# Attention and MLP on one core: the first loads in a fixed order, and the first batch's keys and queries summed, scaled and split through TensorE and ScalarE

## The chip, the cores and the metric

The kernel runs on one core of a Trainium2 chip. The metric is the device time of one execution in microseconds (us), the median of several runs. One profiled execution gives the trace that is read here.

## The reference, cut to what matters

```
def _attn_ref(q, k, v):                     # 4 batches, 8 heads, 576 positions, 64 wide
    q_rot, k_rot = (rotate(q), rotate(k))   # [x1*cos - x2*sin, x1*sin + x2*cos]
    scores = scale * np.matmul(q_rot, k_rot.transpose(0, 1, 3, 2))
    ...                                     # softmax over the last axis
    return np.matmul(attn, v)

def _moe_ref(x, w_in, w_out):               # x: 2304 x 512, w_in: 512 x 2048, w_out: 2048 x 512
    h = x @ w_in
    g = np.where(pos, h, np.where(neg, 0.0, (h + beta) ** 2 / (4.0 * beta)))
    return g @ w_out
```

Keys and queries are rotated by their position, attention is taken for each batch and head, and its output, with the heads side by side, goes through a two-layer MLP.

## The kernel before

Every operand of a product is held as two f16 halves: `hi` is the scaled f32 value rounded to f16, `lo` is what is left. A product is three f16 matmuls (hi x hi, hi x lo, lo x hi). The halves are made by `split`: ScalarE (ACT) writes `hi` = scale * x, then VectorE (DVE) writes `lo` = scale * x - `hi`. The scale of a batch's keys and queries comes from a sum of squares: ACT squares a key tile (`add_square`), a one-column f32 matmul adds the partitions up (`root`), and some one-column DVE steps turn that into the factors (`factors`).

The rotation is done with two copies of each input that the host lays out: x, and x with its halves of 64 rolled. `turn` multiplies the first by the cosines, the second by the sines (both from the table `rt`), and adds the second to the first: three DVE instructions.

The first batch is prepared in four parts, `j` = 0 to 3, each a pair of heads: the keys are `rk[:, j]` (128 x 576, with the rolled copy in a stretch of `w` that is still free, called `first`), the queries `rq[:, j]` (128 x 256). From then on an item is one pair of heads by 128 query rows: 12 matmuls into `psS` (scores), two maxima on DVE (`mx`), two exponentials on ACT (`p`), then `hi` of the two probability tiles on ACT and `lo` on DVE (`phl`), a transposing DMA into `pT`, and later 28 matmuls per pair of items with the values (`psV`). The MLP follows block by block: `psH` from `w_in`, the activation on ACT and DVE (`a`, `r`, `g`), `psO` from `w_out`.

The 16 pieces of the two weight matrices arrive in a 64-bit format, 1 MB each. DVE puts each together with three instructions of 1024 columns (L493, L495, L497), ACT writes `hi`, and for the first five pairs of pieces TensorE (PE) and ACT make `lo`: an f32 matmul against the identity, a second one that subtracts `hi`, both in `psO` (L522, L523), and an ACT copy out of it (L526). The raw pieces use stretches of `w` itself, in the order of `rawseq`.

What order the instructions have on each engine is decided by `Plan.order`: each step has a cost, the steps are laid out in time engine by engine, and of the steps that are ready the one with the smallest rank goes first. The rank is a due time from `wanted`, moved by the table `SLACK` by group of steps. The plain loads go through the queue of SyncE (SP), with up to eight in flight, the raw weights through that of GpSimd (POOL).

Of the kernel before, what the change touches and what calls it, by code (L numbers as in the profile page):

```python
# [10 lines left out]
F32 = mybir.dt.float32  # L11
F16 = mybir.dt.float16
BF16 = mybir.dt.bfloat16
U32 = mybir.dt.uint32
AF = mybir.ActivationFunctionType
ALU = mybir.AluOpType
# [9 lines left out]
    "k0 dve": 41_100, "k0.00 dve": 46_400, "k1 act": 617_700, "k1 dve": 63_800, "k1.10 dve": 21_800,  # L26
    "k1.12 dve": 13_200, "k1.20 act": 39_400, "k1.20 dve": -4_900, "k1.30 dve": 385_800, "left0 act": -440_200,
    "left0 dve": -34_700, "left0.01 dve": 29_800, "left1 act": -682_100, "left1.20 dve": 4_500,
    "left1.22 dve": -1_000, "left1.32 pe": 57_700, "mlp0 act": -48_700, "mlp0 dve": -56_400, "mlp0 pe": 1_362_600,
    "mlp0.0.1 act": 186_100, "mlp0.0.2 act": 74_000, "mlp0.0.7 act": -87_400, "mlp1 dve": -637_500,  # L30
    "mlp1.1.2 act": -106_800, "mlp1.1.3 act": -122_000, "mlp2 act": -875_300, "mlp2 dve": 47_700,
    "mlp2 pe": 40_700, "mlp2.2.2 act": 1_200, "mlp2.2.3 pe": 45_800, "mlp2.2.4 dve": 63_100, "mlp3 act": -691_900,
    "mlp3 dve": -81_700, "mlp3 pe": -23_800, "mlp3.3.3 pe": 241_700, "mlp3.3.4 pe": 225_400,
    "mlp3.3.7 act": 43_400, "mlp3.3.7 pe": 162_900, "mlp3.4.2 pe": -800, "mlp3.5.1 pe": 65_600,
    "mlp3.5.2 dve": -202_300, "mlp3.5.2 pe": 29_400, "mlp3.5.7 pe": 34_500, "mlp3.6.1 pe": 20_600,
    "mlp3.6.2 pe": 25_500, "mlp3.6.7 pe": 163_600, "mlp3.7.0 pe": 82_200, "mlp3.7.3 pe": -15_800,
    "pv0 dve": -448_200, "pv0 pe": -769_100, "pv1 act": -1_444_600, "pv1 dve": -252_200, "pv1.123 pe": 71_100,
    "pv1.302 pe": -66_700, "q0 act": 100_000, "q0 dve": -18_900, "q0.001 act": -77_800, "q0.003 dve": 48_700,
    "q0.010 dve": 109_300, "q0.012 dve": 36_700, "q1 dve": 44_500, "q1.100 dve": -20_700, "q1.110 dve": 8_500,
    "q1.200 dve": -37_600, "q1.210 act": 52_900, "ql0 dve": -134_800, "ql1 dve": 190_900, "raw k0 sp": -12_600,  # L40
    "raw k0.00 sp": -14_800, "raw k0.01 sp": -368_000, "raw k0.02 sp": -12_000, "raw k0.03 sp": 11_100,
    "raw k1 sp": -1_486_700, "raw q0 sp": -6_000, "raw q0.000 sp": -9_500, "raw q0.002 sp": 50_400,
    "raw q0.003 sp": 221_800, "raw v0.0 sp": 71_700, "raw w.1 pool": -67_500, "s0 act": -70_500,
    "s0 dve": -190_500, "s0.001 dve": -66_100, "s0.003 dve": -18_000, "s0.021 dve": 65_100, "s0.022 act": 55_200,
    "s0.022 sp": 21_200, "s0.023 act": 27_000, "s0.031 act": -118_200, "s1 dve": -166_700, "s1 pe": -550_500,
    "s1.101 act": -14_300, "s1.102 act": -34_500, "s1.110 dve": -25_600, "s1.111 dve": -17_400,
    "s1.112 dve": -6_800, "s1.121 dve": 40_400, "s1.122 act": -77_600, "s1.123 act": -123_500,
# [15 lines left out]
class Plan:  # L63
# [59 lines left out]
    def order(self):  # L123
        steps, users = self.steps, self.users()
        n = len(steps)
        rank = [-1e9 if s[5].startswith("init") else x + SLACK.get(s[5], 0.0) + SLACK.get(s[8], 0.0) for x, s in zip(self.wanted(), steps)]
# [6 lines left out]
        def release(i):  # L133
            eng = steps[i][0]
            t = 0.0
            for d in steps[i][4]:
                by = steps[d][0]
                t = max(t, end[d] + (0.0 if by in DMA_ENGINES else 60.0 if by == eng else 205.0 if by == "pe" else 150.0))
            avail[i] = t + 60.0 * (eng in DMA_ENGINES)
            ready[eng].append(i)  # L140
# [43 lines left out]
def kernel(  # L184
# [63 lines left out]
    ndg = [xL_w[:, 256 + 128 * i:384 + 128 * i].bitcast(BF16) for i in range(2)]  # L248
    xL_keys = [("xL", l, e) for l in range(2) for e in range(2)]
# [6 lines left out]
    psO = [ps.tile([128, 512], F32, name=f"psO{i}") for i in range(2)]  # L256
# [24 lines left out]
    def dma(at, dst, src, r, w, nbytes, eng="sp"):  # L281
        q = nc.sync if eng == "sp" else nc.gpsimd
        plan.add(eng, 600.0 if eng == "sp" else 1000.0, at, lambda: q.dma_start(out=dst, in_=src), r, w, bw=nbytes / 300.0)
# [41 lines left out]
    def turn(at, x, xkeys, y, ykeys, p0, n, rep):  # L325
# [155 lines left out]
    def prep_w(which, c, at):  # L481
# [391 lines left out]
```

## Time and profile before

| | |
|---|---|
| median of 3 runs | 636.85 us (635.79 to 637.43) |
| the profiled execution | 636.13 us, of which its trace spans 634.4 us |
| PE busy | 559.6 us (88%) |
| DVE busy | 510.6 us (80%) |
| ACT busy | 441.5 us (70%) |
| DMA | 91.31 MB |

The profile lists each engine's busy time in the span and in 40 equal slices of it, the groups of instructions by line, what ended the idle time ahead of each instruction, and the chain of work that ended last. A busy PE counts matmuls at whatever clock they ran.

### The profile page before, as it was taken

What the parts mean: (1) busy time and instruction counts of PE and PEld (TensorE: products, weight loads), DVE (VectorE), ACT (ScalarE), POOL (GpSimd) and SP (SyncE); (2) the same over time, 40 slices, a digit from 0 to 9 for tenths busy, and PEclk for the clock granted to TensorE, in tenths of its full rate; (3) what the DMA queues carried; (4) which work ended last, traced back from release to release, by engine and by line L of the source; (5) the groups of instructions that cost most, each with busy time, mean ns of one, the idle gap of its engine ahead of it and who ended that gap; (6) DMA issues with size and microseconds to landing.
All of it is one profiled execution on the core that took longest, in us unless ns stands there. A gap on an engine that the chain in (4) does not pass through costs nothing.

```text
span 634.4 us, 12628 instructions
## 1 busy us (share of the span) xinstructions
PE 559.6 (88%) x5078; PEld 358.7 (57%) x5078; DVE 510.6 (80%) x839; ACT 441.5 (70%) x881; POOL 9.3 (1%) x22
## 2 busy tenths in 40 slices
PE   0146657999889899999999999999999999999996
PEld 0023223566565666665666666666666667666663
DVE  1999989999999899999899789968877684334332
ACT  1478768997989789998777799766777574223221
POOL 2000100000000000000000000000000000000000
PEclk9999788999999999999999999999999999999999
DMA  8997797828699968686668675666464664000000
GB/s 335 389 299 146 260 253 203 179 74 178 136 184 249 211 137 199 122 212 141 119 160 177 106 146 115 100 91 107 91 140 75 117 128 90 1 1 35 1 34 17
DMA packets 188009, 91.31 MB, mean 144 GB/s; under 512 B 170160, under 2 KB 178608, under 8 KB 185904
## 3 DMA queue, kind: packets, MB, share of 16 engines
q1 hardware_dynamic: 185648, 73.74, 55.7%
q0 software_dynamic: 2304, 16.78, 7.4%
q8 instruction: 39, 0.64, 0.4%
q14 instruction: 18, 0.15, 0.1%
HBM read 40.96 MB, written 4.72 MB: 72 GB/s over the span
## 4 chain that ended last, share of the span: by engine, by line
PE 54%; DVE 24%; DMA 11%; ACT 6%; issue 3%; SPq 0%; ACTq 0%; DVEq 0%
PE psO L709 20%; PE psH L679 20%; DMA pT<-phl 9%; PE psV L598 6%; DVE phl L555 5%; PE psS L569 5%; DVE mx L543 4%; ACT phl L553 2%; DMA rk<-in_km_dram 2%; ACT p L545 1%; PE psO L522 1%; DVE g L700 1%; PE psS L581 1%; DVE r L696 1%; DVE dup L330 1%
## 5 line engine op out<-in xcount | busy, mean ns | idle before, releaser
L709 PE MATMUL psO<-w,g 128*128 128x512 f16 x864 | 211.2, 380 | 1.2 <-ACT g L698 0.9
L679 PEld LDWEIGHTS <-w 128*128 128x128 f16 x1920 | 171.2, 98 | 48.2 <-issue 6.2
L679 PE MATMUL psH<-xT,w 128*128 128x256 f16 x1536 | 188.8, 273 | 3.2 <-ACT a L686 2.2
L555 DVE SCALAR_TENSOR_TENSOR phl<-p,sums,phl 128x576 f16<-128x576 f32 x144 | 113.4, 812 | 18.1 <-ACT phl L553 17.6
L553 ACT ACTIVATE phl<-p,sums 128x576 f16<-128x576 f32 x144 | 106.7, 766 | 30.6 <-DMA pT<-phl 17.3
L545 ACT ACTIVATE p<-psS,mx 128x576 f32<-128x576 f32 x144 | 105.4, 733 | 29.1 <-DVE mx L543 25.8
L709 PEld LDWEIGHTS <-g 128*128 128x128 f16 x864 | 78.8, 98 | 75.8 <-issue 3.2
L543 DVE TENSOR_REDUCE mx<-psS 128x1 f32<-128x576 f32 x144 | 103.8, 748 | 3.5 <-PE psS L569 2.2
L700 DVE SCALAR_TENSOR_TENSOR g<-r,g 128x512 f16<-128x512 f32 x72 | 49.4, 686 | 52.6 <-ACT g L698 51.5
L569 PE MATMUL psS<-kT,qT 64*128 64x512 f16 (+1 forms) x768 | 68.1, 300 | 19.5 <-ACT p L545 17.4
L686 ACT ACTIVATE a<-psH 128x512 f32<-128x512 f32 x72 | 42.4, 589 | 60.5 <-PE psH L679 60.1
L569 PEld LDWEIGHTS <-qT 64*128 64x128 f16 x768 | 32.5, 97 | 64.8 <-issue 43.4
L698 ACT ACTIVATE g<-r 128x512 f16<-128x512 f32 x72 | 44.9, 623 | 28.1 <-PE psO L709 17.1
L598 PE MATMUL psV<-pT,vS 128*64 128x256 f16 (+1 forms) x768 | 49.5, 251 | 4.1 <-DMA pT<-phl 4.1
L696 DVE SCALAR_TENSOR_TENSOR r<-a,r 128x512 f32<-128x512 f32 x72 | 49.5, 687 | 0.9
L689 DVE SCALAR_TENSOR_TENSOR r<-a 128x512 f32<-128x512 f32 x48 | 33.1, 689 | 19.7 <-ACT a L686 18.8
L598 PEld LDWEIGHTS <-vS 128*64 128x64 f16 x768 | 33.0, 111 | 16.0 <-issue 14.2
L298 PE MATMUL psV<-ssk,ones 128*128 128x1 f32 (+1 forms) x14 | 3.4, 314 | 29.3 <-ACT w L292 28.9
L598 PE MATMUL psV<-pT,vM 128*64 128x256 f16 (+1 forms) x480 | 28.5, 249 | 0.0
L545 ACT ACTIVATION_READ_ACCUMULATOR p<-psS,mx 128x1 f32 x144 | 28.0, 194 | 0.0
L679 PE MATMUL psH<-xL,w 128*128 128x128 f16 x384 | 26.2, 219 | 0.0
L598 PEld LDWEIGHTS <-vM 128*64 128x64 f16 x480 | 21.9, 112 | 0.1
(98 smaller groups left out, 476.7 us busy)
## 6 DMA issues: line engine op xcount, KB each, us to landing
w<-in_w_in_dram POOLq DMA_DIRECT2D x7, 1024.0 KB, 7.5
w<-in_w_out_dram POOLq DMA_DIRECT2D x6, 1024.0 KB, 7.9
rv<-in_vm_dram SPq DMA_DIRECT2D x8, 512.0 KB, 6.2
out_dram<-o SPq DMA_DIRECT2D x16, 256.0 KB, 2.4
rq<-in_qm_dram SPq DMA_DIRECT2D x7, 512.0 KB, 5.0
dup<-in_qm_dram SPq DMA_DIRECT2D x7, 512.0 KB, 4.0
rk<-in_km_dram SPq DMA_DIRECT2D x6, 576.0 KB, 5.1
dup<-in_km_dram SPq DMA_DIRECT2D x6, 576.0 KB, 5.4
```

The costliest lines, as they stand in the source:

```text
L543: plan.add("dve", dve_cost(S, psum=True), at, lambda m=m, src=src: nc.vector.tensor_reduce(out=m, in_=src, op=ALU.max, axis=AX.X, negate=T ...
L545: plan.add("act", act_cost(S, psum=True, ptrs=2), at, lambda a=a, e=e, m=m, src=src: nc.scalar.activation(out=p32[e], in_=src, func=AF.Exp ...
L553: plan.add("act", act_cost(S), at, lambda a=a, e=e, hi=hi: nc.scalar.activation(out=hi, in_=p32[e], func=AF.Copy, scale=rr[:, a:a + 1]), r ...
L555: plan.add("dve", dve_cost(S, ptrs=1), at, lambda a=a, e=e, hi=hi, lo=lo: nc.vector.scalar_tensor_tensor(out=lo, in0=p32[e], scalar=rr[:, ...
L569: nc.tensor.matmul(out=psS[a][:, lo:hi], lhsT=qT[hf][d, l, j, c:c + 128], rhs=kT[ks][d, j, m, lo:hi], start=z == 0, stop=z == 2)
L598: nc.tensor.matmul(out=outs[a], lhsT=st, rhs=moving(a, blk), start=z == 0, stop=z == len(seq) - 1)
L679: nc.tensor.matmul(out=psH[:, n * i:n * i + n], lhsT=wi[ft // 2][:, wl, kk, 128 * (ft % 2):128 * (ft % 2) + 128], rhs=xfn(xl, kk), start=z ...
L686: plan.add("act", act_cost(512, psum=True, ptrs=0), at, lambda one=one: nc.scalar.activation(out=a, in_=psH, func=AF.Relu, scale=2.0 ** -7 ...
L696: plan.add("dve", dve_cost(512), at, lambda one=one: nc.vector.scalar_tensor_tensor(out=r, in0=a, scalar=one, in1=r, op0=ALU.max, op1=ALU. ...
L698: plan.add("act", act_cost(512, ptrs=0), at, lambda g=g, one=one: nc.scalar.activation(out=g[:, 0], in_=r, func=AF.Relu, scale=1.0, bias=- ...
L700: plan.add("dve", dve_cost(512), at, lambda g=g, one=one: nc.vector.scalar_tensor_tensor(out=g[:, 1], in0=r, scalar=-one, in1=g[:, 0], op0 ...
L709: nc.tensor.matmul(out=psO[pos[tt]], lhsT=g[:, gl, n * i + 128 * tt:n * i + 128 * tt + 128], rhs=wo[ft // 2][:, wl, ft % 2, :], start=ft = ...
```

## The change

The four loads of each part `j` (keys, their rolled copy, queries, their rolled copy) get the group name `first`, and so do the values; `order` gives steps of the groups `first` and `raw w` a rank by their place in the code, ahead of everything else. The first four raw weight pieces go through SP's queue, behind the values; the other twelve stay on POOL's queue, in order among themselves (`poolq`).

For the first batch's keys, and the first half of its queries, `turn` leaves the addition out. A diagonal matrix with the factor on it is made by ACT from the identity (`diag`, into the tiles `a` and `r`). `split_pe` then multiplies the two products by that diagonal on PE in f32, one after the other into the same `psO` or `psH`, so that they are summed and scaled there; ACT copies the sum out as `hi`; PE does the same sum again and subtracts `hi` through a negated identity (`nid`); ACT copies the rest out as `lo`. The two `psO` tiles become one tile of 1024 columns, so that 576 fit. The preparation of the values is moved ahead of that of the last 64 query rows (`prep_left`), the square scratch of the weights moves from `r` to `p32[2]`, and the whole table `SLACK` is another one.

```diff
 SLACK = {
-    "k0 dve": 41_100, "k0.00 dve": 46_400, "k1 act": 617_700, "k1 dve": 63_800, "k1.10 dve": 21_800,
+    "k0 act": 23_100, "k0.02 act": -118_400, "k1 act": 521_600, "k1 dve": 42_800, "k1.12 dve": -23_800,
...
-        rank = [-1e9 if s[5].startswith("init") else x + SLACK.get(s[5], 0.0) + SLACK.get(s[8], 0.0) for x, s in zip(self.wanted(), steps)]
+        rank = [x + SLACK.get(s[5], 0.0) + SLACK.get(s[8], 0.0) for x, s in zip(self.wanted(), steps)]
+        rank = [i - 1e9 if s[5].startswith(("init", "first", "raw w")) else rank[i] for i, s in enumerate(steps)]
...
+    nid = xL_w[:, 512:640]
...
-    psO = [ps.tile([128, 512], F32, name=f"psO{i}") for i in range(2)]
+    psO_t = ps.tile([128, 1024], F32, name="psO")
+    psO = [psO_t[:, 512 * i:512 * i + 512] for i in range(2)]
...
+    diags = [[t[:, 128 * j:128 * j + 128] for j in range(NP)] for t in (a_s, r_s)]
+
+    def diag(at, dst, dstkeys, fac):
+        f, fk = fac
+        plan.add("act", act_cost(128), at, lambda: nc.scalar.activation(out=dst, in_=idn, func=AF.Copy, scale=f),
+                 r=[fk, "idn"] + xL_keys, w=dstkeys)
+
+    def split_pe(at, ps, pskeys, dg, dgkeys, parts, hi, hikeys, lo, lokeys, n, done=None):
+
+        cuts = [(c, min(c + 512, n)) for c in range(0, n, 512)]
+
+        def mm(last=True):
+            for c0, c1 in cuts:
+                for z, (x, _) in enumerate(parts):
+                    nc.tensor.matmul(out=ps[:, c0:c1], lhsT=dg, rhs=x[:, c0:c1], start=z == 0, stop=last and z == len(parts) - 1)
+
+        def rest():
+            mm(False)
+            for c0, c1 in cuts:
+                nc.tensor.matmul(out=ps[:, c0:c1], lhsT=nid, rhs=hi[:, c0:c1], start=False, stop=True)
+
+        plan.add("pe", len(parts) * (4 * n / 2.4 + 30), at, mm, r=dgkeys + [k for _, ks in parts for k in ks], w=pskeys)
+        plan.add("act", act_cost(n, psum=True, ptrs=0), at, lambda: nc.scalar.activation(
+            out=hi, in_=ps[:, 0:n], func=AF.Copy), r=pskeys, w=hikeys)
+        plan.add("pe", len(parts) * (4 * n / 2.4 + 30) + pe_cost(1, n) + 60, at, rest,
+                 r=hikeys + xL_keys + ["idn"] + dgkeys + [k for _, ks in parts for k in ks], w=pskeys)
+        plan.add("act", act_cost(n, psum=True, ptrs=0), at, lambda: nc.scalar.activation(
+            out=lo, in_=ps[:, 0:n], func=AF.Copy), r=pskeys, w=lokeys)
...
-        plan.group = f"raw k{min(b, 1)}"
+        plan.group = "raw k1" if b else "first"
...
-        turn(at, x, xk, y, yk, 0, S, n)
+        turn(at, x, xk, y, yk, 0, S, n, b > 0)
...
+        if n == 1:
+            j = js[0]
+            diag(at, diags[0][j], ["a"], kfac[b, j])
+            split_pe(at, psO_t, [("psO", 0), ("psO", 1)], diags[0][j], ["a"],
+                     [(rk[:, j], [("rk", j)]), (second(b, js, S, "k")[0], [("first", j, "k")])],
+                     kT[s][:, j, 0, :], [("kT", s, j, 0)], kT[s][:, j, 1, :], [("kT", s, j, 1)], S)
+            return
...
+        if n == 1 and hf == 0:
+            j = js[0]
+            diag(at, diags[1][j], ["r"], qfac[b, j])
+            split_pe(at, psH, ["psH"], diags[1][j], ["r"],
...
-        plan.group, plan.part = f"raw v{min(b, 1)}", b
+        plan.group, plan.part = "raw v1" if b else "first", b
...
-        dma(at, raw, (w_out if which else w_in).bitcast(U32)[c], [], rk_, 128 * 8192, "pool")
+        dma(at, raw, (w_out if which else w_in).bitcast(U32)[c], [], rk_, 128 * 8192, "sp" if i < 4 else "pool", [] if i < 4 else ["poolq"])
...
+        nc.vector.tensor_scalar(out=nid, in0=idn, scalar1=-1.0, scalar2=None, op0=ALU.mult)
...
+    load_v(0, -8.8)
+    prep_v(0, -8)
     prep_left(0, -5)
-    load_v(0, -8.8)
-    prep_v(0, -4)
```

How the changed table and rules move the first instructions is seen on three engines. In these rows `rk`, `rq_88` and `rv` are keys, queries and values, `w` as a target of a load from `km` or `qm` is a rolled copy, and the number behind a name is a buffer's.

SP's queue from its second load on, before:

```order
L283 DMA rk<-in_km_dram 128x576
L283 DMA w<-in_km_dram 128x576
L283 DMA rk<-in_km_dram 128x576 x2
L283 DMA w<-in_km_dram 128x576 x2
L283 DMA rq_88<-in_qm_dram 128x256
L283 DMA w<-in_qm_dram 128x256
L283 DMA rk<-in_km_dram 128x576
L283 DMA rq_88<-in_qm_dram 128x256
```

and with the change, from part 3's queries on:

```order
L291 DMA rq_88<-in_qm_dram 128x256
L291 DMA w<-in_qm_dram 128x256
L291 DMA rv<-in_vm_dram 128x1024 x2
L291 DMA rvL<-in_vl_dram 64x512
L291 DMA w<-in_w_in_dram 128x2048
L291 DMA w<-in_w_out_dram 128x2048
L291 DMA w<-in_w_in_dram 128x2048
L291 DMA w<-in_w_out_dram 128x2048
L291 DMA rq_89<-in_qm_dram 128x4x256
```

Ahead of these rows the sixteen loads of the four parts stand in order, keys, rolled keys, queries, rolled queries; the first four weight pieces, which were the first loads on POOL, now follow the values on SP.

ACT from its first squares on, before:

```order
L292 ACTIVATE w,ssk<-rk 128x576 x2
L339 ACTIVATE kT_62<-rk,sca 128x576
L292 ACTIVATE w,ssk<-rk 128x576
L292 ACTIVATE r,ssw<-xT_79 128x512 x2
L339 ACTIVATE kT_62<-rk,sca 128x576 x2
```

and with the change, up to the first exponential:

```order
L300 ACTIVATE w,ssk<-rk 128x576 x2
L337 ACTIVATE r<-xL,sca 128x128
L337 ACTIVATE a<-xL,sca 128x128
L300 ACTIVATE w,ssk<-rk 128x576
L355 ACTIVATE qT_64<-psH 128x256
L300 ACTIVATE w,ssk<-rk 128x576
L355 ACTIVATE kT_62<-psO 128x576
L300 ACTIVATE dup_90,ssv<-rv 128x1024
L359 ACTIVATE qT_64<-psH 128x256
L300 ACTIVATE dup_90,ssv<-rv 128x1024
L337 ACTIVATE r<-xL,sca 128x128
L300 ACTIVATE dup_90,ssv<-rvL 64x512
```

The diagonals (L337), both halves (L355 is `hi`, L359 is `lo`) and the squares of the values now stand on ACT ahead of the first item.

PE at its start, before, where the first score matmuls follow the four small sums directly:

```order
L298 MATMUL psV<-ssk,ones 128x1 x4
L569 LDWEIGHTS qT_64
L569 MATMUL psS_112<-kT_62,qT_64 128x512
L569 LDWEIGHTS qT_64
L569 MATMUL psS_113<-kT_62,qT_64 128x512
```

and with the change:

```order
L306 MATMUL psV<-ssk,ones 128x1 x2
L347 MATMUL psH<-rq_88,r 128x256
L347 MATMUL psH<-w,r 128x256
L347 MATMUL psO<-rk,a 128x512
L347 MATMUL psO<-w,a 128x512
L347 MATMUL psO<-rk,a 128x64
L347 MATMUL psO<-w,a 128x64
L306 MATMUL psV<-ssk,ones 128x1
L347 MATMUL psH<-rq_88,r 128x256
L347 MATMUL psH<-w,r 128x256
L352 LDWEIGHTS xL
L352 MATMUL psH<-qT_64,xL 128x256
```

Two f32 passes (L347) per part and operand now stand on PE, the second followed by the f16 subtraction (L352).

## Rows read from the trace of the kernel before

**Rows 1.** The page's busy times and its 40 slices of 15.9 us: each digit is the busy share of a slice in tenths.

```profile
PE 559.6 (88%) x5078; PEld 358.7 (57%) x5078; DVE 510.6 (80%) x839; ACT 441.5 (70%) x881; POOL 9.3 (1%) x22
```

```profile
PE   0146657999889899999999999999999999999996
DVE  1999989999999899999899789968877684334332
```

**Rows 2.** Busy time of each engine in stretches of the span (from:to, length, busy us and count of PE, PEld, DVE, ACT and POOL, then granted clock, DMA share, GB/s).

```profile
0.00:110.00 110.00, 51.78 (x292) 24.70 (x294) 94.38 (x182) 72.77 (x144) 8.11 (x20) 0.92 0.89 270
110.00:260.00 150.00, 140.94 (x1304) 91.34 (x1302) 146.96 (x222) 133.49 (x266) 1.14 (x3) 1.00 0.78 169
260.00:620.00 360.00, 358.41 (x3426) 238.22 (x3421) 266.09 (x433) 232.68 (x470) 0.00 (x0) 1.00 0.52 100
620.00:640.00 20.00, 8.43 (x68) 4.47 (x65) 3.19 (x5) 2.54 (x4) 0.00 (x0) 0.90 0.06 13
...
15.30:58.10 42.80, 16.14 (x78) 8.63 (x79) 42.35 (x107) 29.29 (x66) 1.06 (x2) 1.00 0.95 299
38.60:58.10 19.50, 10.02 (x46) 5.16 (x47) 19.15 (x53) 17.70 (x41) 0.00 (x0) 1.00 0.85 203
```

**Rows 3.** The timeline of the start (start us, busy us, engine, line, operation, then idle time before it and what ended that).

```profile
1.66 0.43 SPq L283 DMA_DIRECT2D w<-in_km_dram  x1
...
10.03 0.76 DVE L330 TENSOR_TENSOR w<-w,rt 128x576 f32<-128x576 f32 x1 [7.44 <-DMA w<-in_km_dram]
...
13.23 1.28 ACT L292 ACT_TABLE_LOAD   x1 [13.23 <-DMA rk<-in_km_dram]
...
15.33 0.76 DVE L328 TENSOR_TENSOR rk<-rk,rt 128x576 f32<-128x576 f32 x1 [4.54 <-ACT w L292]
...
31.78 1.62 PE L569 MATMUL psS<-kT,qT 64*128 64x512 f16 x12 [0.19 <-ACT qT L339]
...
37.18 1.42 ACT L553 ACTIVATE phl<-p,sums 128x576 f16<-128x576 f32 x2
```

```profile
57.52 1.54 DVE L555 SCALAR_TENSOR_TENSOR phl<-p,sums,phl 128x576 f16<-128x576 f32 x2
```

**Rows 4.** What the DMA engines moved in the first stretches of 2 us (the last column is GB/s), and the first loads by group (KB each, median us from issue to landing).

```profile
2.00:4.00 2.00, 0.00 (x0) 0.00 (x0) 0.54 (x2) 0.00 (x0) 2.00 (x5) 1.00 0.91 315
4.00:6.00 2.00, 0.00 (x0) 0.00 (x0) 0.00 (x0) 0.00 (x0) 0.18 (x1) 1.00 1.00 329
6.00:8.00 2.00, 0.00 (x0) 0.00 (x0) 0.00 (x0) 0.00 (x0) 0.00 (x0) 1.00 0.94 344
```

```profile
rk<-in_km_dram SPq DMA_DIRECT2D x4, 288.0 KB, 12.4
...
rt<-in_rot_dram SPq DMA_DIRECT2D x1, 576.0 KB, 3.9
```

**Rows 5.** Pieces of the chain that ended last, in order of time (start us, us, what): the steps of the first preparation as they follow each other on DVE.

```profile
22.92 0.67 DVE w L330
...
31.52 0.34 DVE w L330
31.86 0.40 DVE qT L341
...
37.42 0.73 DVE kT L341
```

**Rows 6.** Groups of DVE instructions, shapes apart (line, engine, operation, out<-in, shape, count, then busy us, mean ns of one, and idle time before).

```profile
L341 DVE SCALAR_TENSOR_TENSOR vS<-rv,sca,vS 128x1024 f16<-128x1024 f32 x8 | 10.2, 1282 | 0.5 <-ACT vS L339 0.5
L332 DVE TENSOR_TENSOR rq<-rq,dup 128x1024 f32<-128x1024 f32 x7 | 8.5, 1215 | 0.0
L495 DVE SCALAR_TENSOR_TENSOR xT<-w,xT 128x1024 uint32<-128x1024 uint32 x7 | 8.5, 1214 | 0.0
L330 DVE TENSOR_TENSOR dup<-dup,rt 128x1152 f32<-128x1152 f32 x6 | 8.1, 1347 | 0.0
L493 DVE TENSOR_SCALAR xT<-w 128x1024 uint32<-128x1024 uint32 x7 | 4.8, 682 | 0.0
L341 DVE SCALAR_TENSOR_TENSOR qT<-rq,sca,qT 128x256 f16<-128x256 f32 x8 | 3.7, 474 | 0.0
L459 DVE SCALAR_TENSOR_TENSOR vZ<-rvL,sca,vM 64x512 f16<-64x512 f32 x4 | 2.9, 736 | 0.0
L510 DVE TENSOR_SCALAR xL<-xL,sca 128x128 bf16<-128x128 f32 x2 | 0.6, 282 | 0.0
```

**Rows 7.** PE's timeline where the weights' f32 matmuls stand. One f32 matmul of 512 columns has two records, "x2".

```profile
55.61 2.07 PE L522 MATMUL psO<-xT,xL 128*128 128x512 f32 x2
57.48 0.63 PE L523 MATMUL psO<-w,xL 128*128 128x512 f16 x1
...
60.60 1.02 PE L522 MATMUL psO<-o,xL 128*128 128x512 f32 x2
61.46 0.38 PE L523 MATMUL psO<-w,xL 128*128 128x512 f16 x1
```

```profile
72.96 2.05 PE L522 MATMUL psO<-o,xL 128*128 128x512 f32 x2 [4.61 <-DVE o L497]
```

**Rows 8.** Groups of ACT instructions, shapes apart, as in rows 6.

```profile
L545 ACT ACTIVATE p<-psS,mx 128x576 f32<-128x576 f32 x144 | 105.4, 733 | 29.1 <-DVE mx L543 25.8 <-DVE phl L555 2.9 <-ACT p L545 0.2
L526 ACT ACTIVATE w<-psO,sca 128x512 f16<-128x512 f32 x20 | 13.5, 681 | 1.4 <-PE psO L523 1.2
L339 ACT ACTIVATE qT<-rq,sca 128x256 f16<-128x256 f32 x8 | 3.8, 497 | 1.8 <-DVE rq L332 1.8
L339 ACT ACTIVATE qL<-rqL,sca 64x64 f16<-64x64 f32 x8 | 2.7, 342 | 0.1
```

**Rows 9.** Who waited for the transposing DMAs, over the span (us, times).

```profile
ACT phl L553: 17.3, 12
```

More of the change, by code (lines that the diff above doesn't have):

```diff
@@ L31 @@
[L31 to L35, printed above, removed]
@@ new lines @@
+    "left1 dve": -164_700, "left1 pe": 22_200, "left1.10 act": 67_800, "left1.10 pe": -32_600,
+    "left1.12 dve": 109_800, "left1.30 pe": -65_700, "left1.32 act": -43_800, "left1.32 pe": 27_300,
+    "mlp0 act": 149_500, "mlp0 dve": -285_900, "mlp0 pe": 575_300, "mlp0.0.5 act": -26_100, "mlp1 act": 53_400,
+    "mlp1 dve": -751_700, "mlp1 pe": 17_500, "mlp1.1.3 act": -15_600, "mlp1.1.4 pe": -73_700,
+    "mlp1.1.5 pe": 130_100, "mlp2 pe": 151_500, "mlp2.2.5 pe": 41_500, "mlp3 pe": -4_300, "mlp3 sp": 59_600,
@@ new lines @@
+    "mlp3.3.2 act": 33_700, "mlp3.3.5 pe": 46_400, "mlp3.3.6 pe": -53_500, "mlp3.3.7 pe": 38_100,
+    "mlp3.4.1 pe": 147_000, "mlp3.4.3 pe": 39_000, "mlp3.5.1 act": -17_700, "mlp3.5.1 pe": -185_700,
+    "mlp3.5.2 pe": -6_700, "mlp3.5.4 pe": -97_400, "mlp3.5.7 sp": 68_800, "mlp3.6.0 pe": 109_700,
+    "mlp3.6.2 pe": 170_900, "mlp3.6.3 pe": -9_900, "mlp3.6.4 pe": -191_200, "mlp3.6.6 pe": -95_400,
+    "mlp3.7.2 pe": -98_200, "mlp3.7.3 pe": 307_100, "mlp3.8.1 pe": 36_200, "mlp3.8.4 pe": 18_300,
@@ new lines @@
+    "s1.233 pe": 16_400, "s1.313 pe": 134_600, "s1.320 dve": -26_400, "s1.323 dve": -136_500,
+    "s1.331 pe": -141_400, "s1.332 pe": 109_500, "scale0 dve": -1_325_200, "scale1 act": 460_900,
+    "scale1 dve": -27_000, "scale1.10 dve": 13_500, "scale1.30 pe": 34_900, "v0 act": -288_800,
+    "v0 dve": -1_217_000, "v1 pe": -292_000, "v1.2 act": -47_200, "v1.2 dve": 90_100, "w act": 86_200,
+    "w dve": 6_700, "w pe": 130_100, "w.0 act": -30_800, "w.3 pe": -117_400, "w.4 dve": 48_700, "w.5 dve": 1_500,
@@ L53 @@
+    "w.6 dve": 21_700,
 }
@@ L137, in release @@
                 by = steps[d][0]
+                if by == eng == "pool":
+                    t = max(t, start[d] + steps[d][1])
+                    continue
                 t = max(t, end[d] + (0.0 if by in DMA_ENGINES else 60.0 if by == eng else 205.0 if by == "pe" else 150.0))
@@ L279, in scalar, with dma @@
         return sca[:, nsca[0] - 1:nsca[0]], ("sca", nsca[0])
-    def dma(at, dst, src, r, w, nbytes, eng="sp"):
+    def dma(at, dst, src, r, w, nbytes, eng="sp", chain=[]):
         q = nc.sync if eng == "sp" else nc.gpsimd
-        plan.add(eng, 600.0 if eng == "sp" else 1000.0, at, lambda: q.dma_start(out=dst, in_=src), r, w, bw=nbytes / 300.0)
+        plan.add(eng, 600.0 if eng == "sp" else 1000.0, at, lambda: q.dma_start(out=dst, in_=src), r, w + chain, bw=nbytes / 400.0)
     def dmaT(at, dst, src, r, w, nbytes):
@@ L331, in turn @@
                  r=["rt"] + ykeys, w=ykeys)
[L332 to L333 removed]
+        if add:
+            plan.add("dve", dve_cost(rep * n), at, lambda: nc.vector.tensor_tensor(out=x, in0=x, in1=y, op=ALU.add),
+                     r=xkeys + ykeys, w=xkeys)
     def split(at, hi, hikeys, lo, lokeys, x, xkeys, fac, n, lo_p=0, np_=128):
@@ L400, in load_q @@
         plan.part = f"{b}{hf}{js[0]}"
-        plan.group = f"raw q{min(b, 1)}"
+        plan.group = "first" if b == 0 and n == 1 else f"raw q{min(b, 1)}"
         dma(at, x, qm[0, b][:, js[0]:js[0] + n, 256 * hf:256 * hf + 256], [], xk, 128 * 4 * n * 256)
@@ L410, in split_q @@
         plan.group = f"q{min(b, 1)}"
+        if n == 1 and hf == 0:
+            j = js[0]
+            diag(at, diags[1][j], ["r"], qfac[b, j])
+            split_pe(at, psH, ["psH"], diags[1][j], ["r"],
+                     [(rq[i][:, j], [("rq", i, j)]), (second(b, js, 256, "q")[0], [("first", j, "q")])],
+                     qT[hf][:, 0, j], [("qT", hf, j, 0)], qT[hf][:, 1, j], [("qT", hf, j, 1)], 256)
+            return
         hi, lo = [qT[hf][:, l, js[0]:js[0] + n, :] for l in range(2)]
```

41 lines of the change are left out of this document (15 added, 26 removed).

## Prediction

> **What bounds the kernel now.** I read the busy times by slice first [rows 1]. From the eighth slice on PE is at eight tenths or more throughout, and DVE is there from the second slice to the twenty-second. So the end is set by PE's list, and how early PE can run that list without gaps is set by DVE, which has to prepare keys, queries, values and weights and do half of each softmax item. The busy times by stretch put numbers to it [rows 2]: PE is idle for 110 - 51.8 = 58.2 us of the first 110, for 9.1 us from 110 to 260, 1.6 us from there to 620, and 6.0 us of the tail. Only the first two can be moved. DVE in the first 110 us is idle for 15.6 us, and the timeline says when [rows 3]: until 10.03 us it waits for the first rolled keys, and 4.54 us more for ACT's squares, which wait for a key load that is there at 13.23. From 15.3 to 58.1 it is idle for 0.45 us [rows 2]. So the start is bounded by the loads up to 15 us and by DVE after that, and a microsecond of DVE work taken out there lets PE's full stretch begin a microsecond earlier.
>
> **The loads.** The first 4 MB of weights now come behind keys, queries and values, in the same 16 engines. The rotation table, part 0 and the second keys are 576 + 3 x 288 + 2 x 128 = 1696 KB (1.74 MB). At the 315 to 344 GB/s of the first stretches [rows 4] with 0.1 MB moved by 2 us they are through at 7.1 us; with a microsecond to land I take 8 against 13.2. An issue on SP takes 0.43 us [rows 3], six of them are out by 3.2 us, so the queue doesn't set this. Bounds: 5 (the table alone took 3.9 us) and 13. The weight pieces are the price: all data ahead of them is 6.2 MB and each piece 1.05 MB, so at some 400 GB/s the four land between 21 and 28 us. The order puts DVE's first work on them behind all the first products, at some 22 us, so this hides; if it didn't, each microsecond of lateness would be one of DVE.
>
> **DVE.** Removed are four additions of 576 and of 256 columns and four `lo` of each: 4 x (0.67 + 0.34 + 0.73 + 0.40) = 8.6 us as they follow each other on the chain [rows 5]. Added is one 128 x 128 negation at 0.28 us [rows 6], in the idle start. So 8.4 us net.
>
> **PE.** A 512-column f32 matmul takes 0.86 us from its start to the next one's at the high clock (60.60 to 61.46) and 1.87 at the low one (55.61 to 57.48) [rows 7]. I take 256 columns as half and 64 as 0.3, estimates. A key pass is 2 x (0.86 + 0.3) = 2.3 us, a query pass 0.86; two of each and the f16 subtractions make 6.8 us a part, 27 us in all, or about 58 at the low clock. They lie in PE's 58 us of early idle time; what counts is that they stand on the path to the first items.
>
> **ACT.** It loses nothing, since `hi` stays; it gains four `lo` of keys and of queries and eight diagonals. No row shows a 576-column copy out of `psO`; between the 512-column one (0.68) and the exponential (0.73, with its sum) [rows 8], less the 0.08 by which neighbours overlap, I take 0.66, for 256 columns 0.40 (the row from SBUF is 0.50), for a diagonal 0.34 (between 0.34 and 0.50, less the overlap). That is 4 x 1.06 + 8 x 0.34 = 7 us.
>
> **The walk to the first item.** First keys landed at 5.5, table load 1.28, two squares until 8.9 (the second waits for the second keys), the sum and factors until 10.4, two diagonals until 11.1. PE starts its first f32 pass there, at the low clock: queries 1.9 us, keys until about 16 if the clock rises during them, as it did between the matmuls at 55.61 and 60.60 [rows 7]; second passes until 20. `lo` of the first keys stands behind the values' squares on ACT, so it is there at 22. First scores at 22.3, against 31.78 [rows 3]. Bounds 18 (no wait on ACT, high clock) and 31 (low clock throughout).
>
> **From the first to the fourth item** the head start is spent. The first `hi` pair of `phl` ends at about 31 against 38.6 [rows 3]. From there to the fourth pair ACT now has six exponentials (0.71), six `hi` of `phl` (0.70), five key halves (0.66), four query halves (0.40), three diagonals, eight 64 x 64 pieces (0.27), four squares (0.75) and 4.4 us of other small pieces: 24 us, where before 17.7 were done in 19.5 [rows 2]. ACT is the bound there. With 3 us of waits, two of them for the last query rows, which DVE now turns later, the fourth pair ends at 58 and its `lo` at 59.5; before, 59.06 [rows 3]. Waits are bounded by 1 and 8 us: the ACT copies out of `psO` waited 0.06 us each on PE on average [rows 8], but here each half waits for a pass of up to 2.8 us.
>
> **Where DVE stands then.** By its order it has, at that point, done work that it had still ahead before: both value `lo` (1.28), four query `lo` of 256 columns (0.47), two 1024-column products, one weight piece's three steps, one 1152-column product and `vZ`, 12.1 us by [rows 6] and 11.1 without the overlaps. It is behind by one maximum and two 128 x 128 steps, 1.1 us. So it is 10.0 us ahead in work and 0.4 us late in time: 9.6 us. (8.4 us of this is the work removed, the rest idle time.) After that the attention has fewer things in its way: ACT's `phl` waited 17.3 us for transposes over the span [rows 9], and by the new order the values are prepared before the second item. I count nothing for it, since DVE had other work in that time.
>
> **Sum.** 636.13 for the profiled execution, less 9.6, is 626.5. The median shown is 0.7 above that execution: 627.2, so 627. The new order table touches all the later stages, too; there PE has 9.1 us of gaps to win from and can lose as much, and I take zero.
>
> **Rivals.** *The start is shorter than my walk.* If ACT waits for nothing in the front and DVE starts at 6 us, DVE's idle time falls by 4.5 us more, and half of PE's gaps from 110 to 260 close: 627 - 9 = 618. Against it: ACT's 24 us are work, not waiting. *Nothing is left of it.* PE's saturated stretch is set by the new table; if its gaps there double, the 9 us are given back: 636. For it: all rows after the front move. Against it: DVE has 8.4 us less to do and is full until 260. *PE stays at the low clock (slower).* The splits go to and fro between PE and ACT through one `psO` and one `psH`, so PE has gaps after each pass. The trace shows what that does: after 4.61 us of waiting the same matmul took 2.05 us instead of 1.02 [rows 7], and the first one of all, at 55.61, took 2.07; I go by these durations. If all passes ran at it, PE's list up to the fourth item is 58 + 4 x 2.3 + 4 = 71 us from 11 us on (2.3 us is an estimate for the score matmuls of an item, from the 1.62 of the first [rows 3] up), with 4 us of waits the fourth pair ends at 86 instead of 58, and the time is 627 + 28 = 655 at worst, about 640 where DVE's queue still has other work to give. In my walk PE has 9 us of slack in that stretch, so the sign turns when about two thirds of the 27 us run at the low clock. Against it: PE is asked for over four fifths of the time between 11 and 58 us.
>
> The Trainium skill, page "TensorE: Matmul & The Clock Gate", section on the HAM clock gate, has the low clock of 1.2 GHz as the default state, which sustained work lifts and idle time brings back; by it a PE that starts f32 passes cold and pauses for ACT between them may stay there, which is this rival and its 640 to 655. The trace agrees with the rule at 55.61, 60.60 and 72.96 us [rows 7]; how gaps of a pass's length act, no row shows.
>
> **Chances.** The forecast (faster by 4 to 14 us) 0.57, the short start 0.08, a gain of 2 to 4 us 0.09; nothing left 0.09; the low clock or worse handoffs, slower, 0.17. A measurement here tells 0.3%, about 1.9 us, from no change. Faster 0.74, same 0.09, slower 0.17. The range leaves out the worst of the low clock and the best of the short start: 616 to 638.
>
> **What would show it.** Right: first scores at 20 to 25 us, the fourth `phl` pair at 56 to 62, PE busy some 25 us more in all and idle by about 35 less, DVE busy near 500, f32 passes of 512 columns near 1.0 us from about 16 us on. Wrong: 512-column f32 records of 2 us beyond 30 us, ACT idle on PE for more than 8 us before the fourth item, DVE waiting for a weight piece, or new PE gaps beyond 110 us.

## The result and the profile after

The change makes the kernel slower by 1.3%: the ratio to the kernel before is 1.013 (95% interval 1.0096 to 1.0163), and the profiled execution took 642.0 us against 636.13. The six times of the changed kernel lie between 642 and 664 us; the ratio rests on the three lowest (642.0, 641.95, 645.82), whose granted clock was 0.974 to 0.978 on average, against 0.955 to 0.971 in the others.

The page of the changed kernel, busy times and slices of 16 us (PEclk is the granted clock in tenths), answers to [rows 1]:

```profile
PE 587.2 (92%) x5186; PEld 376.1 (59%) x5186; DVE 504.1 (79%) x824; ACT 444.4 (69%) x897; POOL 7.2 (1%) x18
...
PE   3877776998989999999999999999999999999996
...
DVE  5799695898999999999997799676886778634332
...
PEclk9988687999999999999999999999999999999999
```

PE is busy for 27.6 us more and idle for 53.0 us instead of 74.8, so 21.8 less. DVE lost 6.5 us of work, yet its row has holes now (a 6, a 5, an 8 among the fifth to eighth slices) where it had a 9, 8, 9 and 9 before. The stretches, as in [rows 2], changed kernel:

```profile
0.00:110.00 110.00, 75.67 (x376) 39.70 (x378) 87.47 (x166) 75.24 (x156) 4.53 (x13) 0.87 0.97 256
110.00:260.00 150.00, 138.95 (x1266) 89.95 (x1264) 141.01 (x213) 128.22 (x255) 2.63 (x5) 0.99 0.75 169
260.00:620.00 360.00, 357.95 (x3421) 237.58 (x3418) 270.30 (x439) 237.21 (x481) 0.00 (x0) 1.00 0.53 104
```

and from 60 to 120 us, the changed kernel's row first, in a second fence that of the kernel before:

```profile
60.00:120.00 60.00, 42.76 (x225) 20.16 (x225) 45.75 (x64) 38.88 (x74) 2.11 (x4) 0.77 0.82 171
```

```profile
60.00:120.00 60.00, 42.91 (x292) 21.30 (x290) 57.92 (x78) 48.49 (x91) 3.69 (x7) 0.86 0.87 228
```

In these 60 us DVE is idle for 14.25 us, where it was idle for 2.08; by what ended them, 11.1 us of these waits were for ACT, 2.5 us for PE and none for a load. Up to there the change did what was forecast; the timeline of the changed kernel (start, us, then idle time before and what ended it), against [rows 3]:

```profile
5.40 1.28 ACT L300 ACT_TABLE_LOAD   x1 [5.40 <-DMA rk<-in_km_dram]
...
13.04 1.91 PE L347 MATMUL psO<-rk,a 128*128 128x512 f32 x2
...
18.08 1.02 PE L347 MATMUL psO<-rk,a 128*128 128x512 f32 x2
...
23.01 0.91 PE L621 MATMUL psS<-kT,qT 64*128 64x512 f16 x12
...
31.87 1.44 ACT L605 ACTIVATE phl<-p,sums 128x576 f16<-128x576 f32 x2 [2.08 <-DVE sums L602]
...
55.39 14.09 SPq L295 DMA_TRANSPOSE pT<-phl  x2
...
57.95 1.44 ACT L605 ACTIVATE phl<-p,sums 128x576 f16<-128x576 f32 x2 [0.65 <-DVE sums L602]
59.02 1.54 DVE L607 SCALAR_TENSOR_TENSOR phl<-p,sums,phl 128x576 f16<-128x576 f32 x2
59.39 0.53 POOL L291 DMA_DIRECT2D w<-in_w_in_dram  x1 [21.20 <-DVE xT L549]
...
69.87 1.44 ACT L605 ACTIVATE phl<-p,sums 128x576 f16<-128x576 f32 x2 [3.60 <-DMA pT<-phl]
...
70.67 1.55 DVE L607 SCALAR_TENSOR_TENSOR phl<-p,sums,phl 128x576 f16<-128x576 f32 x2 [3.28 <-ACT phl L605]
...
109.33 1.06 PE L650 MATMUL psV<-pT,vS 128*64 128x256 f16 x8 [3.54 <-DMA pT<-phl]
...
112.37 0.69 ACT L665 ACTIVATE xT<-psV,sca 128x512 f16<-128x512 f32 x1 [3.53 <-PE psV L650]
...
113.18 0.17 DVE L602 RECIPROCAL sums<-sums 128x2 f32<-128x2 f32 x1 [5.17 <-ACT sums L600]
```

The keys are there at 5.4, the first scores at 23.0, the fourth pair of `phl` ends on DVE at 60.56. Then a transposing DMA, issued at 55.39, is late. ACT can't write the next `phl` (there are two) until 69.87, DVE behind it until 70.67. At 109.33 it is PE that waited, behind it ACT until 112.37 and DVE until 113.18. These two waits of DVE, 3.28 and 5.17 us, are 8.5 of its 14.25. The chain that ended last says how late they were (start, us, what):

```profile
55.39 14.39 DMA pT<-phl
...
93.98 15.30 DMA pT<-phl
```

In flight beside the first is a 1 MB weight piece on POOL's queue, issued at 59.39 in the rows above; beside the second are two, issued at 92.62 and 98.28. What the DMA engines moved from 55 to 70 us, in 40 slices of 0.375 us:

```profile
GB/s 98 209 369 406 313 284 366 341 317 202 243 309 377 358 274 140 291 318 189 5 8 10 144 530 110 23 44 23 23 23 14 344 658 329 328 328 328 187 283 291
...
w<-in_w_in_dram POOLq DMA_DIRECT2D x1, 1024.0 KB, 10.4
```

From the 20th slice to the 31st, with a transpose and most of the weight piece still to be moved, they move 5 to 144 GB/s in all slices but one. So little isn't a lack of bandwidth; something holds both up. The engines are not idle in it: from 62 to 68.5 us their mean busy share (the column before the last) is 0.92, at 171 GB/s.

```profile
62.00:68.50 6.50, 6.11 (x18) 2.29 (x17) 5.39 (x8) 2.77 (x7) 0.00 (x0) 0.57 0.92 171
```

The packet records of the trace say where the time is: of the 128 packets of 8 KB that POOL's queue began from 55 to 70 us, the median took 0.31 us, but 15 took 2.7 us.

### The profile page after: what moved, and what is told of

Read it like the earlier page. It is cut to its first block, busy times and chain, and to the rows that moved or that the text cites. A ratio compares the mean times of both kernels' runs of the same rounds, so it can differ in the third digit from the quotient of the medians.

```text
span 640.2 us, 12853 instructions
## 1 busy us (share of the span) xinstructions
PE 587.2 (92%) x5186; PEld 376.1 (59%) x5186; DVE 504.1 (79%) x824; ACT 444.4 (69%) x897; POOL 7.2 (1%) x18
## 4 chain that ended last, share of the span: by engine, by line
PE 48%; DVE 23%; DMA 17%; ACT 7%; issue 4%; SPq 0%; ACTq 0%; DVEq 0%
PE psO L761 18%; PE psH L731 16%; DMA pT<-phl 13%; PE psV L650 6%; DVE phl L607 6%; DVE mx L595 5%; PE psS L621 4%; ACT phl L605 2%; DMA rv<-in_vm_dram 2%; DVE g L752 2%; DVE r L748 1%; DVE r L741 1%; PE psO L574 1%; DMA w<-in_km_dram 1%; PE psO L347 1%
## 5 line engine op out<-in xcount | busy, mean ns | idle before, releaser
L761 PEld LDWEIGHTS <-g 128*128 128x128 f16 x864 | 79.3, 98 | 74.8 <-issue 1.6
L621 PE MATMUL psS<-kT,qT 64*128 64x512 f16 (+1 forms) x768 | 61.9, 287 | 10.0 <-ACT p L597 9.8
L621 PEld LDWEIGHTS <-qT 64*128 64x128 f16 x768 | 30.2, 95 | 52.9 <-issue 30.8
L602 DVE RECIPROCAL sums<-sums 128x2 f32<-128x2 f32 (+1 forms) x80 | 12.5, 159 | 12.7 <-ACT sums L600 12.3
```

The lines of the kernel that those rows point to most:

```text
L621: nc.tensor.matmul(out=psS[a][:, lo:hi], lhsT=qT[hf][d, l, j, c:c + 128], rhs=kT[ks][d, j, m, lo:hi], start=z == 0, stop=z == 2)
L761: nc.tensor.matmul(out=psO[pos[tt]], lhsT=g[:, gl, n * i + 128 * tt:n * i + 128 * tt + 128], rhs=wo[ft // 2][:, wl, ft % 2, :], start=ft = ...
```

## The experiments

**The theory.** A transposing DMA and loads on POOL's queue that are in flight together hold each other up. Before, seven of the sixteen weight pieces were issued on POOL by 29.0 us, ahead of the first transpose at 39.6, and the other nine among the transposes, from 63.4 us on; in the changed kernel all twelve that POOL has left are issued from 33.3 us on, among the transposes, the first of which is issued at 34.4. The first load of POOL that falls among transposes, before and then with the change:

```profile
63.42 0.53 POOL L283 DMA_DIRECT2D w<-in_w_in_dram  x1 [33.88 <-DVE xT L497]
```

```profile
33.27 0.67 POOL L291 DMA_DIRECT2D w<-in_w_in_dram  x1 [31.96 <-DVE xT L549]
```

Being in flight together isn't enough: in the changed kernel's trace 14 transposes overlap a weight load of POOL; five of them took over 10 us and eight under 6. In the kernel before ten overlap one, and the longest took 11.1 us. **Rivals:** SP's own plain loads for the second batch stand ahead of the transposes and delay them; or the 8 KB packets of the weights are too coarse to share an engine with; or the new order table has simply made a worse order.

**The twelve pieces on SP's queue** (the orders of PE, ACT and DVE stay word for word those of the changed kernel):

```
-        q = nc.sync if eng == "sp" else nc.gpsimd
+        q = nc.sync
```

> The changed kernel with the twelve later weight loads issued on SP's queue, at the same place of the program; PE, ACT and DVE run the same instructions in the same order. In one queue a weight load and a transpose come one after the other. Collision theory: no transpose takes over 9 us from its own issue, the span falls to 630 to 636 us (less than with the small loads, since each 1 MB ahead of a transpose costs it some 3 us). Queue theory: more lies ahead of the transposes, 641 to 648.

Measured: 627.61 us (627.29 to 629.33), ratio 0.990 (0.987 to 0.993), so 14 us less than the changed kernel, and 1.0% faster than the kernel before. Its stretches:

```profile
0.00:110.00 110.00, 79.38 (x449) 43.34 (x450) 93.67 (x177) 80.46 (x169) 0.70 (x6) 0.92 0.95 261
110.00:260.00 150.00, 144.00 (x1316) 94.53 (x1312) 148.26 (x224) 137.26 (x269) 0.00 (x0) 1.00 0.81 186
...
60.00:120.00 60.00, 46.08 (x310) 23.53 (x310) 57.60 (x83) 50.41 (x95) 0.00 (x0) 0.91 0.90 215
```

DVE's idle time from 60 to 120 us is 2.40 us instead of 14.25. From issue to landing (least, median, most) a transpose between 50 and 120 us took, in the kernel before, in the changed one and then in this one:

```profile
DMA to landing us min/median/max: 4.6/6.4/11.1
```

```profile
DMA to landing us min/median/max: 4.5/6.4/15.3
```

```profile
DMA to landing us min/median/max: 4.6/6.4/9.2
```

The median is the same; the longest are gone, and with them the time. The kernel does better than I expected (its trace spans 625.5 us, not 630 to 636), though a transpose takes over 9 us here, too: 9.2, and 11.2 for the first, issued at 37.2. Nor do loads and transposes of one queue simply take turns: 15 transposes overlap a weight load in this trace, and took 6.8 us on average. (Of the dip in what the DMA engines move, four slices of 0.375 us below 50 GB/s are left in the same stretch.) The order of the compute engines can't be the cause, since it was not touched.

**Nine of these twelve pieces with an eighth of their bytes,** still on POOL's queue (the last three stay whole):

```
+        cut = 256 if 4 <= i < 13 else 2048
-        dma(at, raw, (w_out if which else w_in).bitcast(U32)[c], [], rk_, 128 * 8192, "sp" if i < 4 else "pool", [] if i < 4 else ["poolq"])
+        dma(at, raw[:, 0:cut], (w_out if which else w_in).bitcast(U32)[c][:, 0:cut], [], rk_, 128 * 8192, "sp" if i < 4 else "pool", [] if i < 4 else ["poolq"])
```

> The changed kernel with the nine raw weight pieces 4 to 12 loaded only to an eighth (256 of 2048 columns of each; the rest of the piece is what lay there before, so the product with these weights is not the reference's). Order, instructions and waits are unchanged; 8 MB less goes through POOL's queue. Collision theory (a transposing DMA and a weight load of POOL that are in flight together hold each other up): the transposes that took 14.4 and 15.3 us to land take about 5, DVE's 14 us of idle time between 60 and 120 us falls to 2 to 5, the trace spans 628 to 633 us. Queue theory (the second batch's loads, ahead of the transposes in SP's queue, make them late): no change beyond 2 us, 638 to 641.

Measured: 626.09 us (625.02 to 626.21), ratio 0.987 (0.984 to 0.989). The trace spans 624.3 us, less than I expected, and DVE is idle for 2.4 us from 60 to 120. Two remedies of different kinds, another queue for the same bytes and fewer bytes on the same queue, come out 1.5 us apart.

**The second batch's loads on SP with an eighth of their bytes,** the weights as in the changed kernel:

```
+        m = 72 if b == 1 else S
-        dma(at, x, km[0, b][:, js[0]:js[0] + n, :], [], xk, 128 * 4 * n * S)
+        dma(at, x[:, :, 0:m], km[0, b][:, js[0]:js[0] + n, 0:m], [], xk, 128 * 4 * n * S)
```

(and so for the rolled copies and the queries).

> The changed kernel with the second batch's keys and queries loaded only to an eighth (the rest of those tiles is what lay there before, so that batch's result is not the reference's). SP's queue carries some 4 MB less between 20 and 80 us, the order is the same. Queue theory: the transposes after 49 us start earlier and land some 5 us after the issue, the span falls to 628 to 634 us. Collision theory: the two late transposes still take over 12 us while a weight load is in flight, the span stays at 637 to 641.

Measured: 649.72 us (642.69 to 652.16), ratio 1.023 (1.016 to 1.029). Fewer bytes on SP's queue don't help, so it isn't these loads that the transposes wait for. (The edit also adds two small memsets to DVE's start.) The two late transposes on its chain took no less than the 14.4 and 15.3 us of the changed kernel:

```profile
37.57 25.89 DMA pT<-phl
98.84 15.88 DMA pT<-phl
```

**The twelve pieces in packets of 1 KB** instead of 8 KB (the host lays each piece out so that a row of 8 KB comes as eight of 1 KB):

```
+            src = src.rearrange("p (n x) -> (p n) x", n=8).rearrange("(n p) x -> p n x", p=128)
+            dst = raw.rearrange("p (n x) -> p n x", n=8)
```

> The changed kernel with the twelve later weight pieces laid out by the host so that POOL's loads move 1 KB at a time instead of 8 KB; bytes, order and queues are unchanged. Collision theory in the form that the large packets hold a transpose's many small ones up: the late transposes land within 9 us, span 630 to 636. Collision theory in the form that any load of POOL's queue does it: 638 to 642, as now. Queue theory: as now.

Measured: 654.02 us (652.44 to 656.9), ratio 1.032 (1.027 to 1.036). Finer packets don't help, the longest two on the chain being

```profile
56.09 22.29 DMA pT<-phl
102.54 18.53 DMA pT<-phl
```

so it isn't the size of the packets that has to be mended. Whether 1 KB packets are worse than 8 KB ones is not shown: the changed kernel's own times go up to 664 us.

**The kernel before with its weights on SP,** by the same edit:

> The kernel before with its sixteen weight loads on SyncE's queue in place of GpSimd's; TensorE, VectorE and ScalarE have the same instructions in the same order. Theory (a transposing DMA and a GpSimd load in flight together hold each other up): the kernel before has 10 transposes that overlap such a load, at 7.3 us on average against 5.1 us for the others, some 22 us in sum, and few of them were waited for, so little is to be won: 628 to 636 us, much less than the 14 us that the changed kernel won. Rival (one queue is better in itself, by faster loads in the start): the gain is as large as there, about 2%, 622 us. Against both: the weights ahead of the keys on the same queue delay the start, 640 us or more.

Measured: 633.47 us, ratio 0.998 (0.9962 to 0.9999). The same edit that wins 14 us in the changed kernel wins at most 2.4 us here. So the queue is hardly better in itself. The kernel before has its overlaps, too, but they cost it little; it is in the changed kernel that they fall where they cost 14 us.

**The collision by itself.** All compute is left out; 32 transposes follow one another, each waiting for the one before, alone or with 1 MB loads beside them. This kernel and the next ran once each.

> Not the computation: 32 transposing DMAs of the kernel's size one after the other, each waiting for the one before; eight alone, eight with three weight loads of 1 MB on GpSimd's queue in flight, eight with three such loads while VectorE works without a break, and eight with three such loads on SyncE's own queue between the first of them; then the output rows, filled with zeros. Theory: alone each lands after 5 us (4.5 to 6); with GpSimd's loads some take 10 us or more, whether VectorE works or not; with SyncE's loads none above 9 us. Rival (VectorE's work holds up what GpSimd writes for its loads, and that holds up the transposes): over 10 us only in the third stretch. Rival (the load's bytes alone are in the way): the second, third and fourth stretch alike.

Landing times (least, median, most): eight alone; the one that met six loads on POOL's queue; three with one load each on SP's queue.

```profile
DMA to landing us min/median/max: 4.5/4.5/4.6
...
DMA to landing us min/median/max: 34.8/34.8/34.8
...
DMA to landing us min/median/max: 5.6/6.9/7.6
```

The third stretch didn't become what I had meant: its loads depended only on the landing of the first three and so were issued in the second stretch, and the transposes beside DVE's work stood alone, at 4.5 to 4.9 us. But that answers its question, as DVE had next to nothing to do while the one transpose took 34.8 us. From 40 to 78 us, in slices of 0.95 us:

```profile
GB/s 0 69 131 427 427 390 382 409 431 427 320 190 61 47 67 74 92 81 74 35 37 140 27 27 61 81 108 206 401 286 322 300 294 282 267 197 28 26 151 80
```

The first three loads run at some 400 GB/s; then for 13 us all together move 27 to 140 GB/s, with up to three loads waiting. On SP's queue there was never more than one load beside a transpose, so these three compare with the single load below and say nothing of several.

A second kernel of this kind compares the queues, with one load on POOL, three on POOL (issued 0.36 us after the transpose, DVE multiplying), and three on ACT's queue:

> Not the computation: transposing DMAs of the kernel's size one after the other, two alone, six beside one weight load of 1 MB on GpSimd's queue, eight beside three such loads while VectorE multiplies without a break, eight beside three such loads on ScalarE's queue; then the output rows, filled with zeros. The first such kernel had one transpose that took 34.8 us beside six loads on GpSimd's queue, and 5.6 to 7.6 beside loads on SyncE's own. Theory (GpSimd's queue is what the transposes do not go together with): one load holds one transpose for 8 to 15 us, three loads for 20 us or more, VectorE's work changes nothing, and beside ScalarE's queue no transpose takes over 9 us. Rival (any second queue does it): beside ScalarE's queue 10 us or more as well.

The transpose that met the loads took, in this order:

```profile
DMA to landing us min/median/max: 7.9/7.9/7.9
...
DMA to landing us min/median/max: 21.7/21.7/21.7
...
DMA to landing us min/median/max: 12.4/12.4/12.4
```

and the three loads themselves, on POOL's queue and then on ACT's:

```profile
DMA to landing us min/median/max: 15.8/17.9/20.0
...
DMA to landing us min/median/max: 5.2/7.5/9.8
```

One load does little here (7.9 us, where I expected 8 to 15). On ACT's queue, where I expected no transpose over 9 us, three loads take up to 9.8 us and the transpose lands 1.5 us after the last of them: it simply comes last, and the sum of both, 9.8 + 4.6 = 14.4 us, isn't exceeded. So a second queue can delay a transpose to the end of its loads whichever it is (that much of the rival is right), but beside POOL's the loads took twice as long as well, 20.0 us, and the transpose's 21.7 exceed that sum. That pair differs in two things, as DVE multiplied beside POOL's loads and not beside ACT's; that DVE's work isn't needed for a late transpose rests on the 34.8 us above. And a single load, which does little here, was beside a transpose of 14.4 us in the changed kernel; what else it takes is not shown.

**Which part of the change wins.** With all loads on SP I undid one part at a time (`loads`: the fixed order without the split on PE; `split`: the split on PE without the fixed order), each with the new order table, then with that of before, and last the whole change with the table of before.

```
-    "k0 act": 23_100, "k0.02 act": -118_400, "k1 act": 521_600, "k1 dve": 42_800, "k1.12 dve": -23_800,
+    "k0 dve": 41_100, "k0.00 dve": 46_400, "k1 act": 617_700, "k1 dve": 63_800, "k1.10 dve": 21_800,
...
-        rank = [i - 1e9 if s[5].startswith(("init", "first", "raw w")) else rank[i] for i, s in enumerate(steps)]
+        rank = [i - 1e9 if s[5].startswith("init") else rank[i] for i, s in enumerate(steps)]
...
-        turn(at, x, xk, y, yk, 0, S, n, b > 0)
+        turn(at, x, xk, y, yk, 0, S, n)
```

> The changed kernel with its order of loads and its table, all loads on SyncE's queue, but the first keys and queries added and split by VectorE as before. Theory: the earlier keys save up to 5 us of VectorE's idle start and VectorE keeps its 8.4 us of work: 630 to 636 us, beside 627 with both. Rival (the earlier loads are the whole gain, the split on TensorE gives nothing): 627 us.

> The changed kernel with the split on TensorE and its table, all loads on SyncE's queue, but the first loads and weights ordered by due times as before. Theory: VectorE has 8.4 us less to do but starts as late as before: 627 to 633 us. Rival (the split on TensorE gives nothing without the early loads, since it waits for the same keys): 634 us or more.

> The changed kernel with all weight loads on SyncE's queue and the order table of before. If the table of the change is worth little: 627 to 631 us. If the gain hangs on a table made for it: 640 to 655 us, as the two halves of the change (645 and 655) under a table not made for them.

> The order of loads alone, all on SyncE's queue, with the table of before. If the table explains the 645 us under the new one: 629 to 636 us, the earlier keys being worth up to 5 us. If the fixed order of loads is itself harmful without the split: 640 us or more.

> The split on TensorE alone, all loads on SyncE's queue, loads by due times, with the table of before. If the table explains the 655 us under the new one: 628 to 636 us, VectorE's 8.4 us being worth up to that. If the split is itself harmful when the loads come late: 645 us or more.

| all loads on SP | new table | table of before |
|---|---|---|
| both parts | 627.61 | 657.25 |
| order of loads alone | 645.32 | 664.98 |
| split on PE alone | 654.81 | 658.85 |
| neither | not run | 633.47 |

No part came out where I had it if it were worth something by itself (627 to 636 us), and the whole with the table of before is above both of its expectations. The two cells in which the table is that kernel's own are the two fast ones; everywhere else the time is 18 to 37 us over 627.6, more than the parts could bring. For the whole change, where nothing but the table differs, the other table costs 29.6 us. Whether a part is harmful without the other, as some of the expectations put the slow outcome, can't be told from that; what each is worth with an order of its own stays open. It also says that the table wasn't the fault of the changed kernel: with the weight loads on SP it gives the best time of these.

## Why the prediction was wrong

- **Loads: right in what counts.** First keys landed before 5.4 us, forecast 5.5. The four early weight pieces landed between 23.2 and 30.8 us (21 to 28), and DVE waited for none of them. The 6.2 MB ahead of them was a wrong sum; the loads in front of them come to 5.2 MB.
- **DVE, ACT and PE work: about right, one match in part by luck.** DVE has 6.5 us less (8.4 forecast; the terms of that sum give 8.3). ACT's new copies and diagonals take 7.2 us (7), though its busy time rose by only 2.9. PE has 27.6 us more (27), but with all loads on SP, at a higher granted clock, it is 21.2, so part of that match is the low clock. PE's idle time fell by 21.8 us, where my sign of being right was about 35.
- **The walk: right, a little optimistic.** First scores 23.0 (22.3), first pair of `phl` on ACT at 33.3 (31), fourth pair 59.4 and its `lo` 60.6 (58 and 59.5).
- **The low clock as rival: its sign came, but it did not decide.** The splits' 512-column f32 matmul took 1.91 us at 13.04 and 1.02 at 18.08, as walked. But records of 2 us beyond 30 us, my sign of being wrong, came four times between 64 and 102 us, in the weights' matmuls, and from 60 to 120 us the granted clock was 0.77 on average (0.86 before, 0.91 with all loads on SP). The first of them:

```profile
62.14 2.32 PE L621 MATMUL psS<-kT,qT 64*128 64x512 f16 x12 [4.06 <-ACT p L597]
64.39 2.07 PE L574 MATMUL psO<-o,xL 128*128 128x512 f32 x2
```

  Here PE had been idle for 4.06 us, and no late transpose had been waited for yet. With all loads on SP the same stretch is at a low clock as well: from 60 to 70 us it was 0.68 there and 0.66 in the changed kernel.

  By the Trainium skill, "TensorE: Matmul & The Clock Gate", section on the HAM clock gate, idle time brings the clock back down; the trace agrees at 62.14, where twelve score matmuls took 2.32 us behind that idle time and 0.91 at 23.01. As the kernel with all loads on SP has the same splits and is fast, their low clock isn't what cost the time. How much of the lost time passed through a clock that fell behind the late transposes isn't separated.
- **The step that failed** stands under "Where DVE stands then": "After that the attention has fewer things in its way ... I count nothing for it, since DVE had other work in that time." The waits of ACT on transposes, 17.3 us over the span [rows 9], I took as a thing that could only shrink, and entered at nothing in the sum. ACT's did shrink, in the changed kernel and more in the one with all loads on SP (us, times, longest):

```profile
ACT phl L605 <- DMA pT<-phl: 14.5, 10, 3.6
```

```profile
ACT phl L605 <- DMA pT<-phl: 5.5, 5, 2.1
```

  PE's grew, from 4.1 us in four waits before to 8.8 us in eight. And a sum of waits doesn't say whether anything hides them. In the kernel before DVE was busy for 57.9 of 60 us through them, while the longest transpose took 11.1 us; in the changed one two on the chain took 14.4 and 15.3 us, the next steps in DVE's order needed what came behind them, and it stood idle for 14.25 of 60 us. What was left out cost some 15 us and turned the forecast gain of 9.6 into a loss.
- **What I left out of the sum.** Of the sixteen weight pieces I priced the four that moved to SP and asked whether they would be late for DVE. Of the twelve that stay on POOL's queue I did not ask when they are issued now, and what is in flight beside them. The chance of 0.17 that I gave to a slower kernel was for the low clock or worse handoffs, not for this.
- **The sum without that.** With all loads on SP the time is 627.6 us, and 627 was forecast. That nearness is in part luck: the kernel before, run beside it, took 634.5, so the gain is 6.9 us and not 9.6. The loss can be followed on DVE: against that kernel the changed one has 14.25 - 2.40 = 11.9 us more idle time from 60 to 120 us, and from 120 to 260 us, taking the rows of 110 to 120 us below off the stretches above, 4.8 - 1.7 = 3.1 us more; together 15.0, and the profiled times, 642.0 and 627.29, differ by 14.7.

```profile
110.00:120.00 10.00, 8.84 (x69) 5.71 (x66) 5.85 (x9) 4.90 (x11) 0.00 (x0) 0.90 0.20 41
```

```profile
110.00:120.00 10.00, 9.36 (x81) 5.84 (x77) 10.00 (x17) 10.00 (x19) 0.00 (x0) 1.00 0.93 203
```

That the waits and DVE's idle time belong to weight loads on POOL's queue beside transposes is shown by two independent remedies, under which the engines' orders stay the same. Why the two slow each other inside the DMA engines, and why only some of the overlaps do, isn't shown by any run.

## What to carry to other kernels

When loads are moved, ask for every load, the untouched ones too, what is in flight beside it at its new time; on a chain of transposing DMAs with two buffers, a few late ones decide, and the median doesn't show them. Where megabyte loads on a second queue fall among transposes, try them on the transposes' own queue: here it won 14 us in one kernel and at most 2.4 in the other. And an order table that belongs to one kernel can cost more on a variant than the variant can win (29.6 us here), so a part of a change isn't measured by undoing it under a table made for the whole.

## What was not expected of the hardware

- A transpose that takes 4.5 us alone took 34.8 us beside six 1 MB loads on POOL's queue and 21.7 beside three, and the three loads took 20.0 us instead of the 9.8 on ACT's queue (one execution each, DVE at work beside the three on POOL's). The Trainium skill, "DMA: Bandwidth & Descriptors", section "Rules for kernel authors", says of which transfers must wait for each other that "A transpose next to ordinary DMAs needs nothing". That is about the data; of the time it says nothing there, and these runs show that time can be lost.
- During such a collision the DMA engines as a whole move as little as 5 to 144 GB/s in the kernel and 27 to 140 in the kernel of transposes alone, with megabytes waiting. In the GB/s row that looks like idleness, but single packets are held: of the six loads' 768 packets of 8 KB the median took 0.31 us and the longest 7.2.
- Smaller packets on POOL's queue (1 KB for 8 KB) did not shorten the collisions: the longest took 22.3 us there and 15.4 in the changed kernel.
